# A convolution-and-gate block, forward and backward: g kept in SBUF, and forward spectra with real and imaginary parts on the partition rows

## The chip, the core and the metric

One Trainium2 chip, and one of its cores. The metric is the device time of one execution of the program in microseconds, from start to end. The kernel before took 626.39 us (median of 3 runs, 625.23 to 627.68).

## What is computed

The forward pass takes `x` (2048 rows of 512 numbers) through a layer norm, then through two branches whose results are multiplied:

```python
xn = layernorm(x)
K  = real(einsum("dn,dnl,dn->dl", C, exp(dt*A*l), dt*B))   # a filter of 2048 taps per channel
y  = irfft(rfft(pad(xn)) * rfft(pad(K)))[:2048]            # long convolution, one per channel
s  = y + xn * Dskip
g  = silu(silu(xn @ w1) @ w2)                              # w1 512 x 1792, w2 1792 x 512
out = x + s * g
```

The program returns `out` and the gradients of all inputs for a given `grad_out`. So backward passes follow: of the gate, of the two matrix products (`w1`, `w2`, and their input), of the convolution (by spectra again), of the filter's parameters, and of the layer norm.

## The kernel before, in words

**Blocks.** The 512 channels are four blocks `b` of 128. The convolution of a block uses discrete Fourier transforms of length 4096, written as matrix products in two steps. The forward transform is `dft_fwd` (L639): 32 matmuls with the table `TF` (L652), evacuations to SBUF (tile `dA`), 32 transposes (L661, or a transposing DMA), then the second step with the small table `F2` (L671). The inverse is `dft_inv` (L677): the table `I2` (L688), then `TI` (L696).

**Layout of a spectrum.** `F2` is a block of 64 output columns for the real part and 64 for the imaginary part. In the kernel before, L671 makes one part at a time, with 64 output columns, so that two such matmuls (`h` = 0 and 1) use the two column halves of TensorE's array. A spectrum then lies in SBUF as `[64 h + m, part, ...]`: both parts of a number on the same partition, beside each other in the free dimension. `I2` is applied with 64 contraction rows at a time (L688), two matmuls on the two row halves of the array.

**The forward convolution.** `gen_conv_x` (L887) makes the spectrum U of `xn` and stores it in DRAM (`Ud`). `gen_conv_fwd` (L896) loads the filter block `Kb`, makes its spectrum KX, loads U (`spectrum_in`, L881), stores KX (`KXd`), and forms the four products of parts in `cplx_parts` (L718): four instructions on VectorE (L722 to L725), whose four terms `dft_inv` adds up in PSUM. `consume` adds the skip term and makes S, which is stored (`Sd`, L917); the last block's S also stays on chip as `k.S_b`.

**Feed-forward and gates.** `gen_ffn_fwd` (L922) makes the two matrix products in 8 chunks of 256 rows (L936, L955). `gen_gate_rows` (L966) makes `g` = silu of a chunk (L990), stores it in DRAM (`Gd`, L991) and forms `ds` (gradient times g, L992); in a second pass it forms `do` (the gradient times the derivative of silu, L999 and L1000) and multiplies it by s of the first three blocks (L1002). The last block's columns are multiplied at L1550. `gen_out` (L1008) later loads S and g again and forms `x + s g` (L1029, L1030) beside the backward.

**Backward.** `gen_conv_bwd` (L1037) transforms `ds` forward (half-array matmuls as above), loads U and KX, multiplies with `cplx_mul` (L703: L707 to L712) and transforms back twice per block. `gen_ffn_da` (L1265) makes the gradients through w2 and w1 (L1298, L1308). Then come the gradients of the filter's parameters, of w2 (L1346) and of w1 (L1367).

**Order.** The program is first written as interleaved generators, which fixes buffers and dependencies. Then a planner (`Plan`, L36) takes all instructions, gives each a cost, and searches for an order on each engine: `solve` simulates the engines and DMA line with priorities from the last round (`back`), `search` (L386) repeats that with random weights and keeps the order with the earliest end, and `apply` nails it down. So an edit anywhere can move instructions everywhere. Each engine runs its list in order; SyncE (SP) issues most DMAs in order as well, and waits for a DMA's conditions hold up those behind it.

**Buffers.** The transforms draw on a pool with tags: `w8` (4 buffers of a spectrum), `t4` (2 buffers of half that; `Kb` and `S_b`) and `cm2` (1). A tile waits until the tile that had its buffer before has been used for the last time.

Of the kernel before, what the change touches and what calls it, by code (L numbers as in the profile page):

```python
# [24 lines left out]
BR, SR = 1.8, 0.5  # L25
# [10 lines left out]
class Plan:  # L36
# [3 lines left out]
    SEM, ROOM = 45.0, 212863  # L40

    def __init__(self, nc, tc):
# [69 lines left out]
        self.dma = ["DMA" in type(x).__name__ or "Dma" in type(x).__name__ for x in self.ins]  # L112

# [99 lines left out]
    def solve(self, age, pen=0.0, hold=None):  # L213
# [7 lines left out]
        line, tables = 0.0, "nesd"  # L221
# [22 lines left out]
        def pick(e):  # L244
            r = ready[e]
            if e != "Activation" or not pen:
                return heapq.heappop(r)[1]
            i = min(range(len(r)), key=lambda i: (r[i][0] + (pen if switch(r[i][1]) else 0.0), r[i][1]))
# [11 lines left out]
        while events:  # L260
# [110 lines left out]
    def search(self, rounds, seed):  # L371
# [5 lines left out]
        for _ in range(rounds):  # L377
            end = self.solve([-t for t in self.back()], draw.choice((2600.0, 4000.0, 6000.0)), end - draw.uniform(25000.0, 60000.0))
            if best is None or end < best[0]:
                best = end, self.plan, self.start  # L380
# [111 lines left out]
def make_consts(k, wp):  # L492
# [69 lines left out]
    k.I2n = const.tile([P, 128], BF16, name="I2n")  # L562
    TS(out=k.I2n[:], in_=k.I2[:, 0].rearrange("p c m -> p (c m)"), scalar=-1.0, op=ALU.mult)
# [77 lines left out]

def dft_fwd(k, w8, U, ev, dma=False):

# [22 lines left out]
    for u in range(2):  # L666
        for c in range(2):
# [9 lines left out]
def dft_inv(k, A2, Y, ev, consume, terms=None):  # L677
# [3 lines left out]
    terms = terms or [(Y[:, c], k.I2[:, c].rearrange("p c m -> p (c m)")) for c in range(2)]  # L681
    for q in range(4):
        ps = pc.tile([P, 2, 4, 32, 4], F32, name="ps_i2", tag="pc")
        for g in range(4):
            for c, (Yc, I2c) in enumerate(terms):
                for h in range(2):
                    hs = slice(64 * h, 64 * h + 64)
                    nc.tensor.matmul(out=ps[:, h, g], lhsT=Yc[hs, 4 * q + g, :], rhs=I2c[hs], start=(c == 0), stop=(c == len(terms) - 1))  # L688
# [27 lines left out]


def cplx_parts(k, w8, a, b):  # L718

    TT = k.nc.vector.tensor_tensor  # L720
    t = w8.tile([P, 16, P], BF16, name="cm4", tag="cm2")
    TT(out=t[:], in0=b[:, 0], in1=a[:, 0], op=ALU.mult)  # L722
    TT(out=b[:, 0], in0=b[:, 0], in1=a[:, 1], op=ALU.mult)
    TT(out=a[:, 0], in0=b[:, 1], in1=a[:, 0], op=ALU.mult)
    TT(out=b[:, 1], in0=b[:, 1], in1=a[:, 1], op=ALU.mult)  # L725
    re, im = (k.I2[:, c].rearrange("p c m -> p (c m)") for c in range(2))
    return [(t, re), (b[:, 0], im), (a[:, 0], im), (b[:, 1], k.I2n[:])]
# [153 lines left out]
def spectrum_in(k, w8, b, which):  # L881
    t = w8.tile([P, 2, 16, P], BF16, name="sp_in", tag="w8")
    k.nc.sync.dma_start(t[:].rearrange("p c g k -> p (c g k)"), {"U": k.Ud, "K": k.KXd}[which][b])
# [3 lines left out]
def gen_conv_x(k, b):  # L887
# [3 lines left out]
    U, _ = yield from dft_fwd(k, dft, lambda t: k.xn[:, t, bs], k.evc)  # L891
# [4 lines left out]
def gen_conv_fwd(k, b):  # L896
# [7 lines left out]
    KX, A2 = yield from dft_fwd(k, dft, lambda t: Kb[:, :, t, :], k.evc)  # L904
# [10 lines left out]
    yield from dft_inv(k, A2, U, k.evc, consume, terms)  # L915
    k.S_b = S
    (nc.scalar if b == 3 else nc.sync).dma_start(k.Sd[b], S[:].rearrange("p t d -> p (t d)"))  # L917
# [48 lines left out]
def gen_gate_rows(k, gp, lag):  # L966
# [5 lines left out]
    for t in range(0, k.T, 4):  # L972
        nc.sync.dma_start(Gr[:, t:t + 4, :], k.g_v[:, t:t + 4, :])
    rows, S = {}, {}

    def load_s(c):
        S[c] = gp.tile([P, 3, 2, P], BF16, name="S", tag="S", bufs=4)
        nc.sync.dma_start(S[c][:].rearrange("p b t d -> p b (t d)"), k.Sd[0:3, :, 256 * c:256 * c + 256].rearrange("b p n -> p b n"))
    for c in range(last):
# [9 lines left out]
        g = gp.tile([P, 2, k.D], BF16, name="g", tag="g", bufs=3)  # L989
        nc.scalar.activation(out=g[:], in_=rows[c], func=ACT.Silu)  # L990
        nc.sync.dma_start(k.Gd[:, ts, :], g[:])  # L991
        TT(out=k.ds[:, ts, :], in0=Gr[:, ts, :], in1=g[:], op=ALU.mult)  # L992
# [3 lines left out]
    for c in range(last):  # L996
# [4 lines left out]
        o3 = o[:, :, 0:3 * P].rearrange("p t (b d) -> p b t d", b=3)  # L1001
        TT(out=o3, in0=o3, in1=S.pop(c)[:], op=ALU.mult)  # L1002
# [5 lines left out]
def gen_out(k, pool):  # L1008
# [3 lines left out]
    n = k.T // 2  # L1012
    rows = lambda ap: ap.rearrange("p t (b d) -> p b t d", b=4)

    def load(c):
        ts = slice(2 * c, 2 * c + 2)
        S = pool.tile([P, 4, 2, P], BF16, name="go_s", tag="go_s", bufs=2)
        nc.sync.dma_start(S[:].rearrange("p b t d -> p b (t d)"), k.Sd[:, :, 256 * c:256 * c + 256].rearrange("b p n -> p b n"))
        g = pool.tile([P, 2, k.D], BF16, name="go_g", tag="go_g", bufs=2)
        nc.sync.dma_start(g[:], k.Gd[:, ts, :])  # L1020
        return S, g
    q = [load(0), load(1)]
    yield
    for c in range(n):
        S, g = q.pop(0)
        x = pool.tile([P, 2, k.D], BF16, name="go_x", tag="go_x", bufs=1)
        nc.sync.dma_start(x[:], k.x_v[:, 2 * c:2 * c + 2, :])
        yield
        TT(out=rows(g[:]), in0=rows(g[:]), in1=S[:], op=ALU.mult)  # L1029
        TT(out=x[:], in0=x[:], in1=g[:], op=ALU.add)  # L1030
        k.st(k.o0_v[:, 2 * c:2 * c + 2, :], x[:])
        if c + 2 < n:
            q.append(load(c + 2))
        yield


def gen_conv_bwd(k):  # L1037
# [10 lines left out]
    def rest(b):  # L1048
# [23 lines left out]
        yield from dft_inv(k, A2, KX, k.evc, consume_dx)  # L1072
        yield
# [191 lines left out]
def gen_ffn_da(k, da):  # L1265
# [11 lines left out]
    for c in range(T // 2):  # L1277
# [27 lines left out]
        for t in range(2):  # L1305
# [5 lines left out]
            if c >= DU_FIRST:  # L1311
                nc.vector.scalar_tensor_tensor(out=du, in0=ps[:], scalar=1.0, in1=du, op0=ALU.mult, op1=ALU.add,
# [112 lines left out]
def kernel(ctx, tc, A_u, A_A_re, A_A_im, A_B_re, A_B_im, A_C_re, A_C_im, A_log_dt, A_Dskip, B_x, B_w1, B_w2, grad_out,  # L1425
# [21 lines left out]
    k.Gd = dr.tile([P, 16, D], BF16, name="Gd")  # L1447
    k.Md = dr.tile([2 * NB, P, (NE + len(Y_EXP)) * 64], BF16, name="Md")
    k.Sd = dr.tile([NB, P, L], BF16, name="Sd")
# [24 lines left out]
    k.p1 = pool("p1", es=es_f)  # L1474
    k.fp = pool("fp", es=es_f)
    YD = pool("yd", side="right").tile([P, 8192], BF16, name="YD")
# [67 lines left out]
    es_g = es_x.enter_context(ExitStack())  # L1544
    gates = gen_gate_rows(k, pool("gate", side="right", es=es_g), 1)

    interleave([gen_conv_fwd(k, 3), ffn, gates], [1, 3, 1])
    for t in (slice(0, 8), slice(8, 16)):
        last = k.do[:, t, 3 * P:4 * P]
        nc.vector.tensor_tensor(out=last, in0=last, in1=k.S_b[:, t], op=ALU.mult)  # L1550
    es_f.close()
    es_g.close()
# [4 lines left out]
    es_o = es_d.enter_context(ExitStack())  # L1557
    go = pool("go", es=es_o)
    turned_in_place(k, k.W2, k.evw)
    bwd = gen_conv_bwd(k)  # L1560
    out = gen_out(k, go)
# [3 lines left out]
    paced(bwd, woven([ffb, out], [2, 1]), BR)  # L1565
    run(out)
    es_o.close()
# [12 lines left out]
    plan.search(27, 10)  # L1580
# [29 lines left out]
```

## Time and profile before

| | |
|---|---|
| median of 3 runs | 626.39 us |
| the profiled execution | 626.98 us, span 625.3 us, mean granted TensorE clock 0.983 |
| instructions in the profile | 15219 |
| DMA | 178884 packets, 149.63 MB, mean 239 GB/s |
| HBM | read 62.26 MB, written 61.47 MB |

How to read the profile: PE is the matmul side of TensorE, PEld its weight loads, DVE VectorE, ACT ScalarE, POOL GpSimd, SP SyncE. The span runs from the first to the last instruction, and the execution's own time holds 1.7 us more. A group's line gives the source line, engine, operation, what it writes and reads, the count, then the busy time in us and the mean of one in ns. A matmul's mean is its latency; matmuls follow each other at a shorter pace. The view of stages gives busy time per engine in a stretch of the span, with the granted clock and the DMA engines' busy share. The chain is followed back from the last instruction to what released each step.

### The profile page before, as it was taken

Reading aid. Unit: us, or ns where it says so; the run is one execution under the profiler, and the core shown is the slowest. Engines: PE = TensorE matmul, PEld = TensorE weight load, DVE = VectorE, ACT = ScalarE, POOL = GpSimd, SP = SyncE. Lnnn points to the kernel's source line nnn. Section 1 sums busy time; section 2 is a strip of 40 time slices with the busy share of each in tenths; the row PEclk is TensorE's granted clock in tenths of the full one; section 3 lists DMA queues with packets and bytes.
Section 4 is the critical chain, followed back from the end, with each engine's and each line's share of the span. In section 5 each row is a group of like instructions: output and inputs, shape, how many; then the busy total and the mean of one; then the engine's idle time right before and its main releaser. Section 6 shows DMA issues by size and latency. Waiting matters only on the chain.

```text
span 625.3 us, 15219 instructions
## 1 busy us (share of the span) xinstructions
PE 556.0 (89%) x6324; PEld 406.2 (65%) x6324; DVE 504.6 (81%) x881; ACT 459.5 (73%) x620; POOL 83.0 (13%) x157
## 2 busy tenths in 40 slices
PE   0158899889999999859999999999799999999997
PEld 0145665658577667556657665766677877776886
DVE  8999999989998733799979787964549798878692
ACT  6988978968989877996978786631867767663443
POOL 6521112010101010100000000010000302020134
PEclk9989999989999999998999999999899999999999
DMA  9574677798748497889699999999999999999973
GB/s 237 208 285 136 211 254 190 291 222 246 253 159 273 180 306 238 325 290 302 146 313 217 332 244 296 269 240 286 252 278 147 272 217 220 183 235 233 254 203 125
DMA packets 178884, 149.63 MB, mean 239 GB/s; under 512 B 105152, under 2 KB 157120, under 8 KB 175232
## 3 DMA queue, kind: packets, MB, share of 16 engines
q1 hardware_dynamic: 165776, 125.85, 75.0%
q0 software_dynamic: 6144, 17.83, 8.2%
q10 hardware_dynamic: 6896, 4.98, 2.6%
q8 instruction: 49, 0.80, 0.5%
q14 instruction: 19, 0.16, 0.1%
HBM read 62.26 MB, written 61.47 MB: 198 GB/s over the span
## 4 chain that ended last, share of the span: by engine, by line
PE 56%; DVE 19%; ACT 16%; DMA 5%; issue 3%; ACTq 1%; POOL 0%; SPq 0%; DVEq 0%
PE ps_w L1367 8%; PE ps_da L1298 7%; PE ps_dx L1308 7%; PE ps_w L1346 5%; ACT dA L402 3%; PE ps_i L688 3%; PE ps_h L936 3%; PE ps_o L955 3%; PE ps_s L671 3%; PE ps_s L652 2%; DVE Tp L1144 2%; PE ps_i L696 2%; PE ps_v L1134 2%; PE psS L1160 2%; PE psS L1156 2%
## 5 line engine op out<-in xcount | busy, mean ns | idle before, releaser
L402 ACT CAST dA<-ps_s 128x1024 bf16<-128x1024 f32 x96 | 95.5, 1040 | 13.9 <-PE ps_s L652 7.0
L936 PE MATMUL ps_h<-XT,W 128*128 128x256 bf16 x448 | 63.0, 282 | 7.2 <-DVE XT L403 5.2
L402 ACT CAST dB<-ps_i 128x1024 bf16<-128x1024 f32 x48 | 47.3, 1030 | 21.3 <-PE ps_i L688 21.1
L955 PE MATMUL ps_o<-W,aT 128*128 128x512 bf16 x224 | 57.0, 385 | 3.1 <-ACT aT L946 2.7
L1346 PE MATMUL ps_w<-YD,a_tok 128*128 128x512 bf16 x224 | 59.4, 379 | 0.0
L1298 PE MATMUL ps_da<-doT,W 128*128 128x256 bf16 x448 | 58.2, 278 | 0.0
L1144 DVE TENSOR_TENSOR Tp<-Vb,Eb 128x1344 bf16<-128x1344 bf16 x64 | 50.7, 852 | 9.1 <-ACT Vb L402 8.5
L1308 PE MATMUL ps_dx<-W,dhT 128*128 128x512 bf16 x224 | 56.2, 380 | 0.0
L936 PEld LDWEIGHTS <-W 128*128 128x128 bf16 x448 | 42.3, 101 | 18.8 <-issue 11.9
L402 ACT CAST Vb<-ps_v 128x672 bf16<-128x672 f32 x64 | 44.3, 743 | 9.7 <-PE ps_v L1134 9.1
L1298 PEld LDWEIGHTS <-W 128*128 128x128 bf16 x448 | 42.3, 99 | 10.9 <-issue 2.7
L1367 PEld LDWEIGHTS <-xn 128*128 128x128 bf16 x448 | 43.8, 98 | 5.3
L1300 DVE TENSOR_TENSOR dhT<-ps_da,dhT 128x512 bf16<-128x512 f32 x56 | 38.0, 686 | 10.4 <-PE ps_da L1298 6.5
L402 ACT CAST o<-ps_w 128x256 bf16<-128x256 f32 (+1 forms) x42 | 18.7, 446 | 33.9 <-PE ps_w L1367 26.3
L1274 ACT ACTIVATE dhT<-dhT 128x2048 bf16<-128x2048 bf16 (+1 forms) x16 | 27.2, 1713 | 15.9 <-DMA dhT<-Hd 8.5
L947 POOL DMA_DIRECT2D Hd<-hT x16 | 16.4, 1023 | 166.8 <-ACT hT L402 166.8
L652 PEld LDWEIGHTS <-TF 128*128 128x128 bf16 x384 | 27.2, 103 | 16.5 <-issue 8.5
L688 PEld LDWEIGHTS <-sp_in 64*128 64x128 bf16 x768 | 27.8, 94 | 15.3 <-issue 8.5
L955 PEld LDWEIGHTS <-aT 128*128 128x128 bf16 x224 | 19.7, 99 | 24.3 <-ACT aT L946 5.7
L402 ACT CAST hT<-ps_h 128x512 bf16<-128x512 f32 x56 | 31.9, 622 | 4.7 <-PE pt_f L661 3.0
L688 PE MATMUL ps_i<-I,sp_in 64*128 64x128 bf16 x640 | 34.0, 218 | 0.9 <-ACT dK L402 0.6
L1308 PEld LDWEIGHTS <-dhT 128*128 128x128 bf16 x224 | 20.0, 98 | 21.9 <-issue 3.7
(237 smaller groups left out, 1325.8 us busy)
## 6 DMA issues: line engine op xcount, KB each, us to landing
Yd<-YD SPq DMA_DIRECT2D x8, 1024.0 KB, 8.4
sp_in<-Ud SPq DMA_DIRECT2D x8, 1024.0 KB, 7.9
h_in<-Hd SPq DMA_DIRECT2D x14, 512.0 KB, 4.8
Ed<-E SPq DMA_DIRECT2D x8, 672.0 KB, 4.5
Eb<-Ed SPq DMA_DIRECT2D x8, 672.0 KB, 5.7
Hd<-hT POOLq DMA_DIRECT2D x8, 512.0 KB, 6.2
Ud<-dA SPq DMA_DIRECT2D x4, 1024.0 KB, 4.8
KXd<-dA SPq DMA_DIRECT2D x4, 1024.0 KB, 5.2
```

The costliest lines, as they stand in the source:

```text
L402: return self.nc.scalar.copy(out=out, in_=in_)
L652: nc.tensor.matmul(out=ps[:, j], lhsT=k.TF[:, 8 * h + j, c, :], rhs=U(8 * h + j), start=True, stop=True)
L688: nc.tensor.matmul(out=ps[:, h, g], lhsT=Yc[hs, 4 * q + g, :], rhs=I2c[hs], start=(c == 0), stop=(c == len(terms) - 1))
L936: nc.tensor.matmul(out=ps[:, j], lhsT=k.W1[:, dk, ft * P:ft * P + P], rhs=XTv[:, :, dk, :], start=(dk == 0), stop=(dk == DK - 1))
L955: nc.tensor.matmul(out=ps[:], lhsT=aT[:, ft, t * P:t * P + P], rhs=k.W2[:, ft, :], start=(ft == 0), stop=(ft == FT - 1))
L1144: k.nc.vector.tensor_tensor(out=Tp[:, c, :, r ^ c].rearrange("p e (q w) a -> p q w e a", w=2), in0=Vb[:, :, c].rearrange("p q w (e a) -> p ...
L1274: nc.scalar.activation(out=dh[:, 0:n], in_=dh[:, 0:n], func=ACT.Derivative_silu)
L1298: nc.tensor.matmul(out=ps[:, j], lhsT=k.W2[:, ft, dk * P:dk * P + P], rhs=dTv[:, :, dk, :], start=(dk == 0), stop=(dk == DK - 1))
L1300: nc.vector.tensor_tensor(out=dh[:, i0:i0 + 2, :], in0=ps[:], in1=dh[:, i0:i0 + 2, :], op=ALU.mult)
L1308: nc.tensor.matmul(out=ps[:], lhsT=dhs[ft // 8][:, ft % 8, t * P:t * P + P], rhs=k.W1[:, :, ft * P:ft * P + P], start=(ft == 0), stop=(ft ...
L1346: nc.tensor.matmul(out=ps[:], lhsT=at[:, t, :], rhs=k.do[:, t, :], start=(t == 0), stop=(t == k.T - 1))
L1367: nc.tensor.matmul(out=ps[:], lhsT=k.xn[:, t, dk * P:dk * P + P], rhs=dh[:, t].rearrange("p j n -> p (j n)"), start=(t == 0), stop=(t == k ...
```

## The change

- **Spectra.** With `packed`, the second step of `dft_fwd` applies all 128 columns of `F2` at once: 8 matmuls of 128 x 128 instead of 16 of 128 x 64. The result has the real part on partitions 0 to 63 and the imaginary part on 64 to 127. The forward transforms of `xn` and of the filter use it; those of `ds` in the backward don't.
- **Products.** KX, U and a copy of U with the two partition halves swapped (`sp_sw`, four loads per block from DRAM, tag `t4`) are multiplied elementwise, again in four instructions on VectorE. `dft_inv` then adds two terms of 128 contraction rows, with `I2d` (`I2` with the sign of the lower half turned) and `I2`, instead of four terms of 64 rows twice. The new `I2d` replaces `I2n`; `cplx_parts` goes.
- **Loads in the backward.** `spectrum_in` brings the stored spectra back into the old layout, with four loads of 64 partitions each instead of one of 128.
- **g and s.** g stays in SBUF (`g8`, new pool `go`). The second gate pass multiplies both `do` and `g8` by s, `finish_rows` does so for the last block's columns and adds x; `gen_out`, the DRAM tensor `Gd` and the last block's store of S go.
- **Planner.** Its costs of half-array matmuls change, it counts 96 ns for a change of PE's tiling, it may prefer matmuls of the present tiling, and it searches 50 rounds with another seed. `BR`, a weight in the interleaving, goes from 1.8 to 1.0. The pools `fp` and `p1` change their order.

```diff
-BR, SR = 1.8, 0.5
+BR, SR = 1.0, 0.5
...
+    def tiling(x):
+        rows, cols = x.tile_size
+        return 0 if rows * cols == P * P else 1 if rows < P else 2
...
-            half = x.tile_size[0] * x.tile_size[1] < P * P
-            return (d if not half else 3.0 if sum(x.tile_position) == 0 else d + 20.0), d + 165.0
+            if self.tiling(x):
+                return (3.0 if sum(x.tile_position) == 0 else 0.487 * self.count(aps[0]) - 10.0), d + 165.0
+            return d, d + 165.0
...
+                    if self.mode[n] != mode:
+                        mode, d, l = self.mode[n], d + self.TURN, l + self.TURN
...
-    k.I2n = const.tile([P, 128], BF16, name="I2n")
-    TS(out=k.I2n[:], in_=k.I2[:, 0].rearrange("p c m -> p (c m)"), scalar=-1.0, op=ALU.mult)
+    k.I2d = const.tile([P, 128], BF16, name="I2d")
+    for p0, sign in ((0, 1.0), (64, -1.0)):
+        TS(out=k.I2d[p0:p0 + 64], in_=k.I2[p0:p0 + 64, 0].rearrange("p c m -> p (c m)"), scalar=sign, op=ALU.mult)
...
+        for v in range(2 if packed else 0):
+            ps = pc.tile([P, 8, P], F32, name="ps_s2", tag="pc")
+            for h in range(2):
+                nc.tensor.matmul(out=ps[:, 4 * h:4 * h + 4], lhsT=k.F2[:].rearrange("p c m -> p (c m)"), rhs=Bv[:, u, v, h],
+                                 start=True, stop=True)
+            ev(A[:, u, 8 * v:8 * v + 8, :], ps[:])
...
+            for h in range(2 if terms else 0):
+                for i, (T, w) in enumerate(zip(terms(q // 2), (k.I2d[:], I2[1]))):
+                    nc.tensor.matmul(out=ps[:, h, g], lhsT=T[:, 8 * (q % 2) + 4 * h + g, :], rhs=w, start=(i == 0), stop=(i == 1))
...
-    k.nc.sync.dma_start(t[:].rearrange("p c g k -> p (c g k)"), {"U": k.Ud, "K": k.KXd}[which][b])
+    src = {"U": k.Ud, "K": k.KXd}[which][b].rearrange("(c m) (q h n) -> c h m q n", c=2, q=4, h=2)
+    for c in range(2):
+        for h in range(2):
+            k.nc.sync.dma_start(t[64 * h:64 * h + 64, c].rearrange("p (q g) k -> p q (g k)", q=4), src[c, h])
...
-    U = spectrum_in(k, dft, b, "U")
+    U = dft.tile([P, 2, 16, P], BF16, name="sp_in", tag="w8")
+    Us = [dft.tile([P, 16, P], BF16, name="sp_sw", tag="t4") for u in range(2)]
+    for u in range(2):
+        us = slice(2048 * u, 2048 * u + 2048)
+        nc.sync.dma_start(U[:, u].rearrange("p g k -> p (g k)"), k.Ud[b][:, us])
+        for p0 in (0, 64):
+            nc.sync.dma_start(Us[u][p0:p0 + 64].rearrange("p g k -> p (g k)"), k.Ud[b][64 - p0:128 - p0, us])
...
-    terms = cplx_parts(k, dft, KX, U)
+    for u in range(2):
+        nc.vector.tensor_tensor(out=U[:, u], in0=U[:, u], in1=KX[:, u], op=ALU.mult)
+        nc.vector.tensor_tensor(out=Us[u][:], in0=Us[u][:], in1=KX[:, u], op=ALU.mult)
...
-    (nc.scalar if b == 3 else nc.sync).dma_start(k.Sd[b], S[:].rearrange("p t d -> p (t d)"))
+    if b < 3:
+        nc.sync.dma_start(k.Sd[b], S[:].rearrange("p t d -> p (t d)"))
...
-        g = gp.tile([P, 2, k.D], BF16, name="g", tag="g", bufs=3)
-        nc.scalar.activation(out=g[:], in_=rows[c], func=ACT.Silu)
-        nc.sync.dma_start(k.Gd[:, ts, :], g[:])
+        g = k.g8[:, ts, :]
+        nc.scalar.activation(out=g, in_=rows[c], func=ACT.Silu)
...
-        o3 = o[:, :, 0:3 * P].rearrange("p t (b d) -> p b t d", b=3)
-        TT(out=o3, in0=o3, in1=S.pop(c)[:], op=ALU.mult)
+        s3 = S.pop(c)
+        for r in (o, k.g8[:, ts, :]):
+            r3 = r[:, :, 0:3 * P].rearrange("p t (b d) -> p b t d", b=3)
+            TT(out=r3, in0=r3, in1=s3[:], op=ALU.mult)
...
+def finish_rows(k, go):
+    for rows in (k.do, k.g8):
+        for t in (slice(0, 8), slice(8, 16)):
+            last = rows[:, t, 3 * P:4 * P]
+            TT(out=last, in0=last, in1=k.S_b[:, t], op=ALU.mult)
+    for c in range(k.T // 2):
+        x = go.tile([P, 2, k.D], BF16, name="go_x", tag="go_x", bufs=2)
+        nc.sync.dma_start(x[:], k.x_v[:, ts, :])
+        TT(out=x[:], in0=x[:], in1=k.g8[:, ts, :], op=ALU.add)
+        k.st(k.o0_v[:, ts, :], x[:])
...
-    plan.search(27, 10)
+    plan.search(50, 1)
```

More of the change, by code (lines that the diff above doesn't have):

```diff
@@ L211, in graph, with solve @@
         self.ahead = succ, begun, wait, groups
-    def solve(self, age, pen=0.0, hold=None):
+    def solve(self, age, pen=0.0, hold=None, turn=0.0):
         N = len(self.ins)
@@ L220, in solve @@
         free = dict.fromkeys(ready, 0.0)
-        line, tables = 0.0, "nesd"
+        line, tables, mode = 0.0, "nesd", 0
         heat, warm = {}, {0: False}
@@ L245, in pick @@
             r = ready[e]
-            if e != "Activation" or not pen:
+            if e == "Activation" and pen:
+                i = min(range(len(r)), key=lambda i: (r[i][0] + (pen if switch(r[i][1]) else 0.0), r[i][1]))
+            elif e == "PE" and turn and self.mode[r[0][1]] != mode:
+                i = min(range(len(r)), key=lambda i: (r[i][0] + (turn if self.mode[r[i][1]] != mode else 0.0), r[i][1]))
+            else:
                 return heapq.heappop(r)[1]
-            i = min(range(len(r)), key=lambda i: (r[i][0] + (pen if switch(r[i][1]) else 0.0), r[i][1]))
             n = r[i][1]
@@ L377, in search @@
         for _ in range(rounds):
-            end = self.solve([-t for t in self.back()], draw.choice((2600.0, 4000.0, 6000.0)), end - draw.uniform(25000.0, 60000.0))
+            end = self.solve([-t for t in self.back()], draw.choice((2600.0, 4000.0, 6000.0)), end - draw.uniform(25000.0, 60000.0),
+                             draw.choice(self.PEN))
             if best is None or end < best[0]:
@@ L680, in dft_inv @@
     out = A2[:].rearrange("p c t (q h g e) -> p q (h g) (c t) e", q=4, h=2, e=4)
-    terms = terms or [(Y[:, c], k.I2[:, c].rearrange("p c m -> p (c m)")) for c in range(2)]
+    I2 = [k.I2[:, c].rearrange("p c m -> p (c m)") for c in range(2)]
     for q in range(4):
@@ L1072, in rest @@
         yield from dft_inv(k, A2, KX, k.evc, consume_dx)
+        k.du_done = b == 3
         yield
@@ L1543 @@
     k.late = True
-    es_g = es_x.enter_context(ExitStack())
-    gates = gen_gate_rows(k, pool("gate", side="right", es=es_g), 1)
+    go = pool("go", side="right", es=es_x)
+    es_r = es_x.enter_context(ExitStack())
+    gates = gen_gate_rows(k, pool("gate", side="right", es=es_r), go, 1)
     interleave([gen_conv_fwd(k, 3), ffn, gates], [1, 3, 1])
-    for t in (slice(0, 8), slice(8, 16)):
-        last = k.do[:, t, 3 * P:4 * P]
-        nc.vector.tensor_tensor(out=last, in0=last, in1=k.S_b[:, t], op=ALU.mult)
+    finish_rows(k, go)
     es_f.close()
-    es_g.close()
+    es_r.close()
     base = dft_pool("dftb", es_x, {"cm2": 1, "w8b": 2}, k.dft, side="right")
@@ L1564 @@
     ffb = gen_ffn_da(k, da)
-    paced(bwd, woven([ffb, out], [2, 1]), BR)
-    run(out)
-    es_o.close()
+    paced(bwd, ffb, BR)
     es_x.close()
```

65 lines of the change are left out of this document (17 added, 48 removed).

## The prediction

> **What bounds the kernel now.** I read the busy shares first, then the chain that ended last, then both by stage.
>
> ```profile
> PE 556.0 (89%) x6324; PEld 406.2 (65%) x6324; DVE 504.6 (81%) x881; ACT 459.5 (73%) x620; POOL 83.0 (13%) x157
> ...
> PE   0158899889999999859999999999799999999997
> ...
> PEclk9989999989999999998999999999899999999999
> ...
> PE 56%; DVE 19%; ACT 16%; DMA 5%; issue 3%; ACTq 1%; POOL 0%; SPq 0%; DVEq 0%
> ```
>
> TensorE (PE) is the busiest engine, yet only 56% of the chain is PE. So the next view is busy time by stage:
>
> ```profile
> core 0: us, PE busy (x) PEld busy (x) DVE busy (x) ACT busy (x) POOL busy (x), PEclk, DMA share, GB/s
> 45.00:195.00 150.00, 136.56 (x1663) 98.58 (x1662) 141.74 (x193) 129.89 (x183) 15.40 (x15) 0.98 0.68 214
> 195.00:223.00 28.00, 27.77 (x320) 18.61 (x319) 20.16 (x27) 25.73 (x35) 2.85 (x4) 1.00 0.71 259
> 223.00:282.00 59.00, 49.24 (x676) 36.30 (x675) 36.14 (x50) 52.55 (x68) 3.68 (x5) 0.98 0.86 287
> 282.00:430.00 148.00, 146.79 (x1608) 98.90 (x1606) 122.56 (x181) 99.80 (x106) 5.43 (x10) 0.98 0.99 263
> 430.00:573.00 143.00, 136.88 (x1557) 103.19 (x1556) 109.34 (x250) 93.77 (x134) 18.23 (x34) 0.99 1.02 229
> ```
>
> From 282 us on (backward passes) PE is full: what PE saves there, the kernel saves. From 45 to 195 us three engines share the load and DVE (141.74 of 150) is fuller than PE. From 195 to 223 PE is full. From 223 to 282, where the last block's convolution, the gates and the turn to the backward meet, ACT is the fullest. The chain says the same, stage by stage:
>
> ```profile
> by line: PE ps_h L936 9.0%; PE ps_o L955 7.9%; ACT dA L402 7.6%; DMA XT<-xn 5.8%; ACT sn L808 5.7%; PE pt_f L661 3.7%; PE ps_s L652 3.6%; issue 3.6%; DVE YD L828 3.5%; DVE AR L826 3.5%; DVE m L827 3.5%; PE ps_k L842 3.4%; ACT hT L402 3.4%;
> by line: PE ps_o L955 23.0%; PE ps_h L936 17.1%; PE ps_s L671 15.8%; PE ps_k L842 13.7%; PE pt_f L661 12.8%; PE ps_s L652 8.0%; ACT aT L946 6.5%; ACT hT L402 4.2%; issue 1.3%; ACT Xr L402 0.1%; ACTq L402 0.1%
> by line: ACT YD L999 13.0%; DMA YD<-Od 12.6%; ACT g L990 10.6%; ACT aT L946 10.4%; ACT dA L402 8.4%; ACT L999 6.5%; ACT dB L402 6.2%; DMA Kd<-KE 6.2%; issue 5.6%; ACTq L877 4.5%; ACT hT L402 4.4%; ACT L990 4.3%; ACT KE L402 4.3%; ACT ob L40
> ```
>
> These are 45–195, 195–223 and 223–282. PE entries sum to 27.6% in the first (9.0+7.9+3.7+3.6+3.4; the line is cut, so it is a lower bound), 90.4% in the second, nothing visible in the third.
>
> **Full-array matmuls: what they save.** Pieces of the chain in order of time (start, us, what):
>
> ```profile
> 361.68 0.16 PE ps_i L688 x2
> 361.85 0.21 PE ps_da L1298
> 362.06 0.94 PE ps_i L688 x30
> ...
> 365.28 1.79 PE ps_i L696 x32
> ...
> 374.36 0.55 PE ps_s L671 x4
> ...
> 376.11 0.54 PE ps_dx L1308 x2
> ...
> 413.26 5.89 PE ps_da L1298 x54
> 419.15 6.04 PE ps_dx L1308 x28
> ```
>
> The paces of full-array matmuls: L696 1.79/32 = 56 ns at 128 columns, L1298 5.89/54 = 109 ns at 256, L1308 6.04/28 = 216 ns at 512. Now the half-array ones. L671 uses half the columns and runs as pairs: 4 of them are two pairs, 2 x 0.216 = 0.43 us, but take 0.55; and two ps_dx ahead of such a run take 0.54 instead of 0.43. Going into half arrays and back costs 0.12 + 0.11 = 0.23 us. L688 uses half the rows: 30 are 15 pairs, 0.84 us at 56 ns, but take 0.94; the one ps_da ahead of it takes 0.21 instead of 0.11. Together 0.20 us per visit. So a half-array pair costs what one full matmul costs, and the arithmetic saves nothing: the diff puts one full matmul (L684, L707 of the new file) where a pair stood. What it saves is the visits.
>
> In the instruction order of the two built programs PE visits half arrays 92 times before (44 of L671's kind, 48 of L688's) and 38 times after (13 and 25), all 38 in the backward. By place, from the order and the start times: 17 and 9 visits in 45–195, 17 x 0.23 + 9 x 0.20 = 5.7 us; 8 and 0 in 195–223, 1.8 us; 3 and 9 in 223–282, 2.5 us; 16 and 30 after 282, of which 13 and 25 stay, 3 x 0.23 + 5 x 0.20 = 1.7 us. All of it is 11.7 us of PE time.
>
> What of it reaches the end: after 282 all, 1.7 (PE full). In 195–223, 90% of 1.8: 1.6. In 45–195 between 27.6% of 5.7 (1.6) and all of it (PE busy 91%, but so is DVE 94%): I take 1.6, because DVE is the fuller engine. In 223–282 nothing to 2.5; I take 0: the chain is ACT there.
>
> **The last block and SP's queue.** Timeline, 244 to 262 us:
>
> ```profile
> 246.93 2.60 SPq L991 DMA_DIRECT2D Gd<-g  x2
> ...
> 249.63 0.58 SPq L883 DMA_DIRECT2D sp_in<-Ud  x1
> ...
> 258.18 1.23 DVE L722 TENSOR_TENSOR cm<-sp_in,dA 128x2048 bf16<-128x2048 bf16 x1 [2.91 <-DMA sp_in<-Ud]
> ```
>
> Before, SP held the last block's load of U 2.6 us behind stores of g that waited for ACT; the product on DVE then waited 2.91 us for that load. With g on chip those stores go. After, i2 can also start when one half's two products are done, not all four. But the loads double: U, and U again with its halves swapped. Prices of the nearest DMAs (KB each, us to landing):
>
> ```profile
> sp_in<-Ud SPq DMA_DIRECT2D x8, 1024.0 KB, 7.9
> ...
> Gd<-g SPq DMA_DIRECT2D x8, 256.0 KB, 5.8
> ...
> go_s<-Sd SPq DMA_DIRECT2D x8, 256.0 KB, 5.3
> ```
>
> Six pieces of 256 to 512 KB instead of one of 1024 KB land between as before (7.9) and twice that (15.8); against it stand 2.6 us and, since the swapped loads wait only for earlier users of their two buffers, an earlier issue. Ends: 2.6 won, 7.9 lost. I take 0, as ACT's queue of Silu and its derivative sets this stretch and not the product. The Trainium skill, page "DMA: Bandwidth & Descriptors", section "Rules for kernel authors", speaks against the change here: it advises not to split a transfer into two partition halves, as they share the same engines and serialize. By it the 15.8 would hold, 7.9 more; no trace here shows the split.
>
> In the backward the same doubt meets 8 loads of spectra, now four pieces of 256 KB each: 7.9 to 4 x 5.3 = 21 us if one after the other. I take 7.9, the row of the same bytes; the cover is ps_da and ps_dx, which keep PE at 146.79 of 148, and without that cover the worst end is 13 us on one load.
>
> **g and s on chip.** Removed: 8 stores and 8 loads of g and 8 loads of s, 256 KB each, and the last block's store of s, 512 KB: 6,656 KB; added 4 x 1,024 KB for the swapped U. SP issues grow by 20 + 24 and shrink by 24. DVE's rows:
>
> ```profile
> L1030 DVE TENSOR_TENSOR go_x<-go_x,go_g 128x1024 bf16<-128x1024 bf16 x8 | 5.5, 683 | 0.0
> L1029 DVE TENSOR_TENSOR go_g<-go_g,go_s 128x1024 bf16<-128x1024 bf16 x8 | 5.5, 683 | 0.7 <-DMA go_g<-Gd 0.7
> L1002 DVE TENSOR_TENSOR YD<-YD,S 128x768 bf16<-128x768 bf16 x8 | 4.3, 549 | 1.2 <-DMA S<-Sd 1.2
> L1550 DVE TENSOR_TENSOR YD<-YD,S_b 128x1024 bf16<-128x1024 bf16 x2 | 1.4, 682 | 0.0
> ```
>
> The 8 products L1029 (5.5 us), spread over the backward, become 8 like L1002 and 2 like L1550 (4.3 + 1.4 = 5.7 us) around the turn. There DVE is busy 36.14 of 59 us, so 23 us of idle hide them; without that cover they cost 5.7. The additions L1030 stay. In the backward DVE had 25 us of idle, so the lighter load gives nothing.
>
> **Sum.** 1.7 + 1.6 + 1.6 = 4.9 us off. The profiled execution took 626.98 us (span 625.3 and 1.7 around it), 0.6 above the median 626.39; so about 622.1 for a like execution and **621.5** for the median. Its own range: 618 to 624.
>
> **Rivals.**
> (a) PE bounds the forward too, since DVE's and ACT's waits there are partly for PE in-order work: all 11.7 us count. 626.4 - 11.7 = 614.7. For it: PE 91% busy in 45–195. Against: DVE 94%.
> (b) The forward is DVE's and ACT's, and only the backward's 1.7 counts: 624.7. For it: the third chain line; against: 90% PE in 195–223.
> (c) The clock. One row shows it at half, after a thin stretch:
>
> ```profile
> 276.00:280.00 4.00, 1.57 (x19) 1.25 (x19) 4.00 (x7) 3.97 (x5) 0.00 (x0) 0.96 0.77 238
> 280.00:286.00 6.00, 4.89 (x33) 3.78 (x31) 5.98 (x12) 6.00 (x7) 0.00 (x0) 0.50 1.00 313
> ```
>
> After 4 us in which PE was busy for 1.57, the granted clock was 0.50 for 6 us: 3 us of work lost. A forward with less PE work could bring one more such stretch: 621.5 + 3 = 624.5. The Trainium skill, "TensorE: Matmul & The Clock Gate", "Why this matters for your kernels", says that an idle window of about 3 us halves the clock; this row agrees, and one more window is not certain.
> (d) Slower: SP's queue, which is in order, stalls on the swapped loads. They wait for buffers that the K block, the swapped U and S share (two buffers), and behind them stand loads that DVE and PE need: in the new order, first of all E's store and the magnitudes of the next tables. Two rows price such a stall, one of SP's waits and one of the chain:
>
> ```profile
> SPq L901 <- DMA Kd<-KE: 46.0, 4, 19.5
> ...
> 97.25 8.70 DMA XT<-xn
> ```
>
> One load that came late cost the chain 8.70. With (b)'s gain, 624.7 + 8.7 = 633; with mine 630. It decides once a swapped load holds SP past the time when DVE runs out of table work. Against it: in 45–195 DVE was idle for only 8 of 150 us, whatever it waited for, with as strict a queue.
> (e) That it doesn't do what it says: the instruction order shows the 54 visits gone, so only their worth is open.
>
> **Chances.** Forecast 0.42, (a) 0.18, (b) 0.17, (c) 0.08, (d) 0.15. The range of 612 to 631 holds all but half of (d) and the tails. A measurement tells 0.5% (3.1 us) from no change: faster means below 623.3, slower above 629.5. Forecast (less a tail of 0.02) and (a) are faster, 0.58; (b), (c) and that tail the same, 0.27; (d) slower, 0.15.
>
> **What would show it.** Right: PE pieces of 56 ns for L707 with no step ahead of them; PE busy lower by about 11 us; the first ps_da 3 us earlier; the backward 1.7 us shorter. Wrong: the product waiting longer than 2.91 us for sp_in or sp_sw; DVE waiting for tables' loads behind the swapped loads; first ps_da no earlier though PE's busy time fell (b); the first ps_da 9 us earlier (a); more half-clock stretches (c).

## The result and the profile after

| | before | after |
|---|---|---|
| runs side by side, median (lowest to highest of 7) | 627.38 us (625.23 to 628.65) | 621.92 us (619.05 to 628.40) |
| ratio, 95% interval | | 0.992 (0.989 to 0.995) |
| profiled execution, span, mean granted clock | 626.98 us, 625.3 us, 0.983 | 621.48 us, 619.8 us, 0.989 |

The forecast was 621.5 us. The changed kernel was timed twice more beside the kernel before (below as c1_after and c2_after): 0.9964 (0.9936 to 0.9992) and 0.9965 (0.9932 to 0.9999). Ratios, here and below, are of the runs in the faster of two states that executions show, medians and ranges of all runs. The three intervals lie below 1, the third only just. So the gain is small, 0.4 to 0.8% by the ratios, some 3 us in their mean; by the medians of the three sets it is 5.5, 1.4 and 0.9 us. Two sets of three lie below the 0.5% that the prediction set as its bound. The number was met; its composition wasn't, as the rest shows.

First the profile page of the kernel after: busy time, PE's and the clock's rows of forty slices, and the chain.

```profile
PE 541.0 (87%) x5958; PEld 407.7 (66%) x6004; DVE 503.3 (81%) x884; ACT 457.8 (74%) x620; POOL 79.7 (13%) x157
...
PE   0139999888999988969999899799999999999998
...
PEclk9999999999999997989999999999999999999999
...
PE 52%; DVE 18%; ACT 15%; DMA 10%; issue 3%; ACTq 1%; POOL 0%; SPq 0%; DVEq 0%
```

PE is 15.0 us less busy, but 46 matmul records are missing here (5958 against 6004 weight loads). The profile of the second repeat, c2_after, has them all:

```profile
PE 544.7 (88%) x6004; PEld 407.8 (66%) x6004; DVE 503.5 (81%) x884; ACT 457.6 (74%) x620; POOL 78.1 (13%) x157
```

Against 556.0 before that is 11.3 us less PE time; 11.7 was predicted. In the chain DMA's share rose from 5% to 10%. The view of stages of after, with bounds moved to its own landmarks (columns as before):

```profile
43.00:193.00 150.00, 138.06 (x1542) 105.47 (x1558) 147.17 (x202) 135.33 (x193) 13.94 (x17) 1.00 0.82 252
193.00:221.00 28.00, 26.78 (x335) 21.41 (x339) 20.95 (x27) 27.46 (x45) 2.27 (x3) 1.00 0.79 257
221.00:276.00 55.00, 43.14 (x477) 33.20 (x478) 37.26 (x55) 46.57 (x52) 2.81 (x4) 0.92 0.93 275
276.00:436.00 160.00, 153.01 (x1664) 104.78 (x1663) 124.08 (x183) 101.93 (x108) 6.51 (x12) 0.99 1.02 230
436.00:567.00 131.00, 125.54 (x1469) 95.71 (x1489) 102.42 (x241) 91.27 (x132) 17.10 (x32) 1.00 1.04 227
```

The first stage is as long as before, starts 2 us earlier and is fuller (DVE 147.17 of 150 us, 141.74 before); the third is 4 us shorter. The fourth has become longer: PE, which was busy for 146.79 of 148 us in the backward before, is now idle for 7 of 160. The turn is easiest to see between two instructions that both kernels have, the first `ps_da` (backward through w2) and the last `ps_dx`. Between them, before and then after:

```profile
282.50:438.20 155.70, 154.49 (x1654) 103.24 (x1653) 124.90 (x185) 100.17 (x106) 5.98 (x11) 0.99 1.00 264
```

```profile
275.40:436.20 160.80, 153.81 (x1667) 105.27 (x1667) 124.88 (x185) 102.53 (x108) 6.51 (x12) 0.98 1.02 229
```

So the backward starts 7.1 us earlier (3.2 predicted) and takes 5.1 us longer (1.7 shorter predicted). Part of the 5.1 is a border: 14 more weight loads lie in this stretch (x1667 for x1653), and the stretch behind it has as many fewer. It is cleaner to take all from the first `ps_da` to the end: 342.8 us before (625.3 - 282.5), 344.4 after (619.8 - 275.4). The rest is PE waiting for DMAs, in the chain of waits of after (276 to 436 us; start, us, what):

```profile
by line: PE ps_da L1311 24.6%; PE ps_dx L1321 22.9%; DMA dhT<-Hd 10.1%; PE ps_i L711 7.0%; DMA Pd<-pd_s 6.5%; PE ps_i L719 4.5%; issue 3.6%; PE ps_s L691 3.1%; PE ps_s L666 2.6%; DVE dhT L1313 1.9%; DVE sp_in L732 1.8%; PE pt_f L675 1.4%; A
...
330.71 8.23 DMA dhT<-Hd
...
339.45 7.90 DMA dhT<-Hd
...
383.39 10.38 DMA Pd<-pd_s
```

### The profile page after: what moved, and what is told of

Read it like the earlier page. It is cut to its first block, busy times and chain, and to the rows that moved or that the text cites. A ratio compares the mean times of both kernels' runs of the same rounds, so it can differ in the third digit from the quotient of the medians.

```text
span 619.8 us, 14576 instructions
## 1 busy us (share of the span) xinstructions
PE 541.0 (87%) x5958; PEld 407.7 (66%) x6004; DVE 503.3 (81%) x884; ACT 457.8 (74%) x620; POOL 79.7 (13%) x157
## 4 chain that ended last, share of the span: by engine, by line
PE 52%; DVE 18%; ACT 15%; DMA 10%; issue 3%; ACTq 1%; POOL 0%; SPq 0%; DVEq 0%
PE ps_w L1381 8%; PE ps_da L1311 6%; PE ps_dx L1321 6%; ACT dA L415 5%; PE ps_w L1360 5%; PE ps_o L978 4%; PE ps_h L959 3%; DMA dhT<-Hd 3%; DMA Kd<-KE 2%; PE psS L1169 2%; PE ps_v L1147 2%; PE ps_i L711 2%; DVE Tp L1157 2%; PE psS L1173 2%; DMA Pd<-pd_s 2%
## 5 line engine op out<-in xcount | busy, mean ns | idle before, releaser
L415 ACT CAST dA<-ps_s 128x1024 bf16<-128x1024 f32 x96 | 94.1, 1056 | 8.4 <-PE ps_s L691 4.2
L959 PE MATMUL ps_h<-XT,W 128*128 128x256 bf16 x448 | 61.5, 285 | 5.9 <-ACT ob L415 3.3
L415 ACT CAST dB<-ps_i 128x1024 bf16<-128x1024 f32 x48 | 47.6, 1028 | 11.8 <-PE ps_i L711 8.6
L978 PE MATMUL ps_o<-W,aT 128*128 128x512 bf16 x208 | 52.8, 379 | 2.3 <-ACT hT L415 1.0
L1360 PE MATMUL ps_w<-YD,a_tok 128*128 128x512 bf16 x202 | 53.3, 379 | 0.8
L959 PEld LDWEIGHTS <-W 128*128 128x128 bf16 x448 | 43.9, 102 | 14.6 <-issue 6.4
L1311 PEld LDWEIGHTS <-W 128*128 128x128 bf16 x448 | 42.6, 99 | 15.3 <-issue 7.2
L1287 ACT ACTIVATE dhT<-dhT 128x2048 bf16<-128x2048 bf16 (+1 forms) x16 | 27.1, 1704 | 13.3 <-DMA dhT<-Hd 13.3
L970 POOL DMA_DIRECT2D Hd<-hT x16 | 14.0, 876 | 150.6 <-ACT hT L415 150.6
L1147 PE MATMUL ps_v<-Gb,YT 128*128 128x168 bf16 x256 | 29.6, 236 | 2.6 <-DMA YT<-Yd 1.1
L819 ACT ACTIVATE sn<-AR 128x2048 bf16<-128x2048 int32 (+1 forms) x16 | 30.5, 1912 | 1.8 <-DVE AR L817 1.8
```

Of the source, the lines that this page charges most:

```text
L415: return self.nc.scalar.copy(out=out, in_=in_)
L819: nc.scalar.activation(out=sn[:, :, 0:n], in_=V[:, :, 0:n], func=ACT.Sin, scale=-2 * PI_LO / 2.0 ** 32)
L959: nc.tensor.matmul(out=ps[:, j], lhsT=k.W1[:, dk, ft * P:ft * P + P], rhs=XTv[:, :, dk, :], start=(dk == 0), stop=(dk == DK - 1))
L978: nc.tensor.matmul(out=ps[:], lhsT=aT[:, ft, t * P:t * P + P], rhs=k.W2[:, ft, :], start=(ft == 0), stop=(ft == FT - 1))
L1147: nc.tensor.matmul(out=ps[:, u, 168 * c:168 * c + 168], lhsT=YT[:, c, q + u, :], rhs=Gb[:, q0 + q + u].rearrange("p w x -> p (w x)"), star ...
L1287: nc.scalar.activation(out=dh[:, 0:n], in_=dh[:, 0:n], func=ACT.Derivative_silu)
```

## Experiments

The theory at first: the visits to half arrays give the gain, at the price and with the shares of the prediction; the backward's loss comes from how its spectra are loaded, or from the order. The rivals: all PE time counts (a); the order that the planner happened to find gives the difference; the removed transfers matter after all.

All results in one table. "Visits" are PE's visits to half arrays ahead of the first `ps_da`, from the instruction order. "First ps_da", "from there" (to the end) and "PE idle" (between first `ps_da` and last `ps_dx`) are of the profiled execution, in us. Ratios are to the kernel before on the same chip; its medians in the three sets were 625.81 (first four rows below c2_after), 625.89 (c1_after, e5 to e7) and 625.61 (c2_after, e8 to e10).

| kernel | visits | first ps_da | from there | PE idle | median | ratio (95%) |
|---|---|---|---|---|---|---|
| before | 46 | 282.5 | 342.8 | 1.2 | | 1 |
| after | 0 | 275.4 | 344.4 | 7.0 | 621.92 | 0.992 (0.989, 0.995) |
| c1_after | 0 | 278.9 | 344.2 | 5.5 | 624.46 | 0.9964 (0.9936, 0.9992) |
| c2_after | 0 | 274.9 | 346.2 | 7.9 | 624.67 | 0.9965 (0.9932, 0.9999) |
| e1_halves | 25 | 276.8 | 349.7 | 7.0 | 628.20 | 1.0034 (1.0015, 1.0053) |
| e2_long | 0 | 274.4 | 345.7 | 6.3 | 621.00 | 0.9937 (0.9903, 0.9971) |
| e3_seed | 0 | 278.8 | 351.6 | 8.1 | 631.37 | 1.0074 (1.0047, 1.0102) |
| e4_planner | 41 | 280.7 | 346.3 | 3.3 | 628.77 | 1.0057 (1.0033, 1.0082) |
| e5_dma | 0 | 275.2 | 354.7 | 15.0 | 629.08 | 1.0054 (1.0029, 1.0080) |
| e6_seed4 | 0 | 285.1 | 339.2 | 3.7 | 623.24 | 0.9964 (0.9940, 0.9987) |
| e7_bseed2 | 50 | 294.1 | 345.2 | 3.0 | 643.23 | 1.0281 (1.0247, 1.0315) |
| e8_halves | 25 | 279.2 | 348.0 | 8.5 | 628.21 | 1.0039 (1.0011, 1.0067) |
| e9_spec | 0 | 273.9 | 349.5 | 9.4 | 623.30 | 0.9957 (0.9932, 0.9982) |
| e10_g | 41 | 297.1 | 336.5 | 2.9 | 635.10 | 1.0132 (1.0100, 1.0163) |

**What a visit costs: e1_halves and e8_halves.** In the order of after, kept as it is, each full matmul of L684 becomes the pair of half-array matmuls that stood there before. The planner plans the first of a pair alone; the second is put behind it when the order is nailed down.

```diff
-                nc.tensor.matmul(out=ps[:, 4 * h:4 * h + 4], lhsT=k.F2[:].rearrange("p c m -> p (c m)"), rhs=Bv[:, u, v, h],
-                                 start=True, stop=True)
+                for c in range(2):
+                    TWINS[c].append(nc.tensor.matmul(out=ps[64 * c:64 * c + 64, 4 * h:4 * h + 4], lhsT=k.F2[:, c, :], rhs=Bv[:, u, v, h],
+                                                     start=True, stop=True))
...
+            line = [y for n in line for y in ([self.ins[n], self.twin[n]] if n in self.twin else [self.ins[n]])]
```

> The kernel after, with its own order of instructions on every engine, in which only the 64 full-array matmuls of the packed second step (L684) are each put back as a pair of half-column matmuls. PE then visits half arrays 25 more times, all in the forward. At 0.23 us a visit that is 5.8 us of PE time. Theory (a visit counts where the chain is on PE): 9 of the 25 places lie on the chain of the kernel after, so about 2 us longer than after, 624. Rival A (PE bounds the whole forward): 5.8 us longer, 627.7. Rival N (visits were hidden anyway, and the new order alone brought the gain): within 0.5 us of after, 622.

> The first experiment again (the kernel after, its own order, 64 matmuls put back as pairs of half-column ones, 25 visits more), this time beside the kernel after itself on the same chip; the two were measured in different sets before, 1.0034 against 0.992 and 0.9964. The traces show each visit at 0.22 us and the first ps_da 1.4 us later. Theory (a visit counts where the chain is on PE): 2 us slower than after in this set. Rival A (all visits count): 5.5 us slower or more.

The same stretch of PE's order, first in c2_after and then in e8_halves, which ran on the same chip (timeline: start, us, what; a group's time runs to its last end, so the pace is read from start to start):

```profile
209.15 0.56 PE L675 MATMUL pt_f<-band,dA 128*128 128x128 bf16 x7
209.54 0.59 PE L684 MATMUL ps_s<-dB,F 128*128 128x512 bf16 x2
209.97 1.25 PE L959 MATMUL ps_h<-XT,W 128*128 128x256 bf16 x10
```

```profile
211.82 0.55 PE L682 MATMUL pt_f<-band,dA 128*128 128x128 bf16 x7
212.31 0.62 PE L692 MATMUL ps_s<-dB,F 128*64 128x512 bf16 x4
212.86 1.27 PE L967 MATMUL ps_h<-XT,W 128*128 128x256 bf16 x10
```

Seven transposes take 0.39 us ahead of full matmuls and 0.49 ahead of half ones; two full matmuls take 0.43 us, the two pairs that do the same work take 0.55. That is 0.10 + 0.12 = 0.22 us per visit, and a pair costs one full matmul. So the price was right (0.23). The Trainium skill, "TensorEngine Tiling (Array Packing)", "Key Properties", says that a change of tiling mode drains TensorE; these two steps agree. For 25 visits it makes 5.5 us of PE time. Of it, 3.5 us reach the end by the medians of one set (628.21 - 624.67) and 4.6 by the two ratios (1.0039 - 0.9965, of 626). In e8_halves 15 of the visits stand ahead of 193 us, 6 between 193 and 221 and 4 behind; by the shares of the prediction (28%, 90%, nothing) 2.1 us would reach the end. The two intervals together leave 4.6 +/- 2.7, so this one pair of runs excludes neither the 2.1 nor all 5.5. e1_halves, the same kernel in another set, gave the same ratio (1.0034), and the three ratios of after lie at 0.992 to 0.9965. The profiles don't say where the cost arises either: from c2_after to e8_halves the first `ps_da` comes 4.3 us later and the rest takes 1.8 us longer, from after to e1_halves it is 1.4 and 5.3, though all 25 visits lie ahead of the first `ps_da`. So the visits do cost time at the end; whether a share of it, as predicted, or all, as in rival (a), these runs don't decide.

**How the backward's spectra are loaded: e2_long.** The loads stay four, but each row of DRAM comes as one run of 4 KB instead of four of 1 KB; the rows' contents stand in another order then.

```diff
-    src = {"U": k.Ud, "K": k.KXd}[which][b].rearrange("(c m) (q h n) -> c h m q n", c=2, q=4, h=2)
+    src = {"U": k.Ud, "K": k.KXd}[which][b].rearrange("(c m) (h q n) -> c h m q n", c=2, q=4, h=2)
```

> The kernel after, with its own order, in which the backward's loads of spectra read runs of 4 KB in place of 1 KB (same number of loads, same bytes, same buffers; the spectra then stand in a wrong order, so the backward's numbers differ). After has 7 us of PE idle between 340 and 436 us that before hasn't, behind late loads of dhT and stores of pd_s. Theory (runs of 1 KB keep the DMA engines busy longer and make the others late): PE idle there falls to 2 us or less, and the time by about 5 us, 617. Rival (the new order of DMA issues makes them late, whatever the runs): same time as after within 1 us.

The ratio is 0.9937, PE's idle time in the backward 6.3 us against 5.5 to 7.9: the length of the runs is not what holds PE. That the spectra come in 32 transfers instead of 8 was not tried by itself.

**The removed transfers: e5_dma.** Into after's order, 21 of the removed transfers are put back beside the backward: seven stores of g (256 KB), seven loads of g (256 KB) and seven of S (192 KB), 4,928 KB in all. Nothing reads what they load.

```diff
+        for d in range(max(c - 1, 0), c):
+            ds = slice(2 * d, 2 * d + 2)
+            TWINS.append(nc.sync.dma_start(k.Gd[:, ds, :], k.g8[:, ds, :]))
+            old = go.tile([P, 2, k.D], BF16, name="go_g", tag="go_g", bufs=1)
+            TWINS.append(nc.sync.dma_start(old[:], k.Gd[:, 0:2, :]))
+            old = go.tile([P, 3, 2, P], BF16, name="go_s", tag="go_s", bufs=1)
+            TWINS.append(nc.sync.dma_start(old[:].rearrange("p b t d -> p b (t d)"), k.Sd[:, :, 256 * d:256 * d + 256].rearrange("b p n -> p b n")))
```

> The kernel after, with its own order, in which seven of the eight sets of DMAs that the change removed are put back into the backward, each behind a load of x: the store of a chunk of g (256 KB, of the product in this kernel), a load of g (256 KB) and a load of s (192 KB), into buffers that nothing reads. That is 21 DMAs, 4.9 MB. Theory (these DMAs are off the path, as the prediction costed them at nothing): within 1 us of after. Rival (the backward's DMA engines are full, and the 7 us of PE idle there come from late transfers, so 4.9 MB more lengthen it): 5 us or more longer, 627 or above.

> The kernel after once more, unchanged, as the mark for the others of this set on their chip. Both theories: 0.992 of before, within the interval of the first measurement, 0.989 to 0.995.

They cost 5.6 us by the two ratios (1.0054 - 0.9964, of 626; the intervals together leave 5.6 +/- 2.4) and 4.6 by the medians (629.08 - 624.46, the control on the same chip). The control itself, c1_after, came out at 0.9964, outside the 0.989 to 0.995 that was expected. The waits of the backward (us in total, times, longest), first after, then e5_dma:

```profile
ACT dhT L1287 <- DMA dhT<-Hd: 13.3, 6, 4.6
...
ACT pd_s L415 <- DMA Pd<-pd_s: 4.1, 1, 4.1
```

```profile
ACT dhT L1300 <- DMA dhT<-Hd: 23.5, 6, 8.0
...
DVE cm L736 <- DMA sp_in<-Ud: 7.8, 2, 6.0
...
DVE cm L736 <- DMA sp_in<-KXd: 5.6, 2, 3.4
```

Where ACT waited 13.3 us for the stored activations (11.8 in c1_after) it now waits 23.5, and the loads of spectra come late as well; PE's idle time goes to 15.0 us. The stretch between the two landmarks is 172.2 us long, 11.6 more than in c1_after, though it began 3.7 us earlier. First c1_after, then e5_dma:

```profile
278.90:439.50 160.60, 155.15 (x1666) 106.37 (x1666) 125.06 (x185) 102.58 (x108) 6.51 (x12) 0.97 1.00 229
```

```profile
275.20:447.40 172.20, 157.19 (x1666) 107.21 (x1666) 125.64 (x185) 102.57 (x108) 6.51 (x12) 0.96 1.03 243
```

The DMA share is 1.03 here and was 1.00 without the extra bytes (1.02 in the profile of after): the DMA engines had no room left, and transfers that no engine waits for still cost time. Other loads land later, as dhT of 512 KB, after 7.1 us in the median against 6.1 in c1_after. A second way stays open: SP issues the 21 in its own order, at some 0.4 us each, and waits five times for one of them to land (us in total, times, longest):

```profile
SPq L1055 <- DMA Gd<-g: 3.2, 1, 3.2
SPq L1057 <- DMA go_s<-Sd: 2.7, 2, 2.0
SPq L1055 <- DMA go_g<-Gd: 1.9, 2, 1.0
```

What stands behind them in SP's queue starts later for that; the runs don't part the two. (This profiled execution took 631.65 us, 2.6 above its kernel's median.)

**The order's luck: e3_seed, e6_seed4, e4_planner, e7_bseed2.** The first two are after with another seed (2, and 4 in e6_seed4):

```diff
-    plan.search(50, 1)
+    plan.search(50, 2)
```

The last two are before with all planner edits of the change and seed 1, or 2 in e7_bseed2:

```diff
-    plan.search(27, 10)
+    plan.search(50, 1)
```

> The kernel after with another seed of the planner's search (2 in place of 1): another order of the same work; 39 visits to half arrays in place of 38. Theory (the gain is in the work that goes): 622 within 3 us, below before in any case. Rival (the gain of 5.5 us is the luck of one order): it may come out at 627 or above.

> The kernel after with seed 4 of the planner's search (40 visits, none in the forward). With seed 2 it was 1.5% slower than with seed 1. Theory now (an order's luck is some 5 us either way, the removed work some 5 to 6 us on the average): between 622 and 632. Rival (seed 1 is typical and seed 2 was the odd one): 622 within 2 us.

> The kernel before with the planner of after (its costs of half arrays, 96 ns for a change of tiling, preference, 50 rounds, seed 1) and nothing else of the change. Visits fall from 92 to 73 (44 to 35 and 48 to 38), 9 x 0.23 + 10 x 0.20 = 4.1 us of PE time, of which 5 and 0 before the first ps_da. Theory (visits count in full only in the backward, in part in the forward): 2 to 3 us faster than before, 624 to 625. Rival (the planner brought the whole gain): 622 or below. Rival (an order's luck outweighs it): 627 or above.

> The kernel before with the planner of after and seed 2 (92 visits, 50 of them in the forward). Theory (removed work on top of an order's luck): like seed 1 of this pairing (1.0057 of before), slower than the mean of the kernel after's seeds: 627 to 637. Rival (the work that goes is worth nothing, all is luck): as fast as the kernel after's seeds, 622 to 627.

The same work in three orders (after, e3, e6) takes 0.992 to 1.0074 of the time; the work of before under the new planner takes 1.0057 and 1.0281. One draw moves the time by as much as the whole change does, and within it the stages trade: e6_seed4 comes to the first `ps_da` at 285.1 us, 6 to 10 us after the other two, and has the shortest rest (339.2). The 7.1 and 5.1 us of the result are inside that spread. The planner by itself shows no gain: both draws are slower than before with its own order. e3_seed and e4_planner went the way of the rival that an order's luck outweighs the change; e6_seed4 lies in both of its ranges; e7_bseed2, at 643.23 us, is slower than the 627 to 637 of its expectation.

**One part alone: e9_spec and e10_g.** Both are before with after's planner and seed 1: e9_spec with the spectra's part (`packed`, products, loads), e10_g with g's (`g8`, `finish_rows`, `BR`, pools).

> The kernel before with the planner of after (seed 1) and the spectra's part of the change alone: full-array matmuls and the swapped loads, while g and s still go through DRAM and the last step beside the backward reads them back. 35 visits, none in the forward. The same planner without it gave 1.0057 and 1.0281 of before with two seeds, the whole change 0.994, 1.0074 and 0.9964 with three. Theory (the visits carry most of the gain): 0.993 to 1.003. Rival (g's DMAs, which are still there, carry it): 1.005 to 1.02.

> The kernel before with the planner of after (seed 1) and g's part of the change alone: g stays on chip and s g is formed at the second gate pass, while the spectra keep the old layout and half-array matmuls. 72 visits, 41 in the forward. Theory (the visits carry most of the gain, and g's DMAs matter only in the order of after): 1.002 to 1.015. Rival (g's DMAs carry it): 0.99 to 1.0.

> The kernel after once more, unchanged, as the mark for this set. So far it stood at 0.992 and at 0.9964 of before in two sets. Both theories: 0.992 to 0.997.

e9_spec is as fast as the whole change (0.9957 beside 0.9965 in the same set); e10_g is slower than before. Sort the kernels by whether their forward visits half arrays: without visits (after, e3, e6, e9) the first `ps_da` comes at 275.4, 278.8, 285.1 and 273.9 us, 278.3 in the mean; with them (before, e4, e7, e10) at 282.5, 280.7, 294.1 and 297.1, 288.6 in the mean. That is 10.3 us for 41 to 50 visits, which at 0.22 us are 9 to 11. From there to the end it is 346.2 us in the mean without and 342.7 with them. Four orders on each side with a spread of 11 and 16 us make that likely, not proved. g's part alone shows no gain in its one draw, although 21 of its transfers cost 5.6 us when they are put back into after's order. One draw each, against a spread of 1.1 to 1.5% between draws of the same work, doesn't rank the two parts.

## Why the prediction was right, and where not

The time was met with steps that were off in opposite directions.

- **The price of a visit** (0.23 and 0.20 us) and the sum of PE time (11.7) held: 0.22 and 11.3. Ahead of the first `ps_da` PE was busy for 223.75 us in before and 213.19 in c2_after, 10.6 less (10.0 predicted), behind it for 332.22 and 331.52, 0.7 less (1.7 predicted). Not all of it is visits: before ran 16 more `ps_h` in the first 45 us, at a pace of 0.21 us instead of 0.11, which makes an estimated 1.6 of the 10.6. Matmuls of the new L707 run at 56 ns with no step, as in this piece of after's chain (0.67/12):

```profile
130.55 0.67 PE ps_i L707 x12
```

- **What reaches the end ahead of the turn (1.6 + 1.6 + 0) was too small.** The first `ps_da` came 7.1, 3.6 and 7.6 us earlier in the three profiles of after, not 3.2. The step that failed is "I take 1.6, because DVE is the fuller engine": in after's first stage DVE was busy for 147.17 of 150 us instead of 141.74, as if part of its idle time had been PE's. That would be rival (a)'s mechanism, for the forward alone, and is argued: the order changed too, in a kept order 25 visits moved the first `ps_da` by 1.4 and 4.3 us, and e6_seed4, without visits, comes to it at 285.1 us, later than before.
- **The backward (1.7 won) has the wrong sign.** From the first `ps_da` on, after needs 1.4 to 3.4 us more than before in its three profiles. "PE full, so all counts" took a stage's occupancy for a bound that would stay; DMA, at a share of 0.99 there, was as full, and PE arrived earlier at it.
- **Removed DMAs at zero** was wrong: e5_dma prices 21 of them at 5.6 us in after's order (4.6 by the medians).
- **The spectra in four pieces at zero** holds for the loads themselves, with the 7.9 us of the prediction. After's row for them, and an issue of four on SP:

```profile
sp_in<-Ud SPq DMA_DIRECT2D x16, 256.0 KB, 6.0
...
sp_in<-KXd SPq DMA_DIRECT2D x16, 256.0 KB, 5.1
```

```profile
334.83 2.67 SPq L897 DMA_DIRECT2D sp_in<-Ud  x4
```

  Four issues take 2.67 us. In after's eight loads the last piece lands 7.4 to 10.4 us after the first issue, 8.1 in the median: near the predicted 7.9, not 21. One whole load in before's backward took 5.2 to 7.8 us, 6.4 in the median, so the four pieces are slower by an estimated 1.7 us. The Trainium skill, "DMA: Bandwidth & Descriptors", "Rules for kernel authors", says that two transfers to disjoint partition halves serialize. A doubling, as the prediction worked out from it for the last block, is not what these loads show. Whether 32 transfers instead of 8 are what lets PE wait longer in every order with packed spectra (3.7 to 9.4 us idle) than in every order without (1.2 to 3.3) stays open: these orders also start the backward earlier, the other explanation, all but e6_seed4, which has the 3.7.
- **The last block, 0,** held. Waits for U ahead of the turn, in before (43 to 282 us) and in after (43 to 276):

```profile
DVE cm L722 <- DMA sp_in<-Ud: 7.3, 2, 4.4
```

```profile
DVE sp_in L929 <- DMA sp_in<-Ud: 2.9, 2, 2.2
```

  No product waits for a swapped load; rival (d) did not come. SP did wait 9.5 us at these loads (5.5 for a store of S, 4.0 for PE), but DVE was busy for 147.17 of 150 us all the same.
- **Rival (c), the clock.** Between 48 us and the last 3 us of the span the clock stood at half for 13.6 us in before, 13.6 in after and 23.8 in c1_after. The prediction takes its row at the turn as agreeing with an idle window of about 3 us. The row doesn't show one: PE was busy for 1.57 of 4 us, its longest gap ahead of the half clock is 1.51 us, and the clock halved all the same. At the turn, after and then c1_after (the column with 0.51 and 0.52 is the granted clock):

```profile
273.80:280.80 7.00, 5.45 (x36) 4.33 (x36) 6.46 (x13) 7.00 (x8) 0.00 (x0) 0.51 1.27 224
```

```profile
274.00:284.60 10.60, 8.41 (x60) 6.89 (x61) 9.83 (x18) 10.57 (x11) 0.00 (x0) 0.52 1.25 241
```

  The same program, so such stretches come and go between executions. The 10.2 us more are 5 us of work, and c1_after's span was 3.3 us longer than after's.
- **The step that the prediction lacked is the order.** It counted the change as edits to one fixed order, while the planner made a new one. The draws above span 1.1 to 1.5% of the time for after's work and 2.8% for before's, more than the 0.8% that was forecast: with the same mechanisms another seed would have given "slower" (e3_seed). The range of 612 to 631 was argued from other causes; after's two other draws lie in it (623.24) and just outside (631.37). That 621.5 was met to 0.4 us is therefore luck in part.

What is shown: 0.22 us per visit on PE, a cost of 25 visits at the end in a kept order (4.6 +/- 2.7 us), 5.6 +/- 2.4 us for 21 transfers, and the spread of the draws. What is argued: that the spectra's part carries the gain (e9_spec beside e10_g and the grouping). Open: how much of the 3 us is the order, and why the backward of after loses time.

## What to carry to other kernels

Price a change of tiling by its visits, not by its matmuls: a pair of half-array matmuls costs one full one, and 0.22 us go for entering and leaving. A stage where PE is full may be one where DMA is just as full, and then neither PE time that is saved nor transfers that nobody waits for can be counted by PE's row alone. Where a search sets the order, first time a few seeds of the kernel as it stands: here they spread by more than the change is worth, and an edit is told from luck only in a kept order or over several seeds.

## What was not expected of the hardware

- The DMA engines' share was 1.02 in the backward of after at 229 GB/s and 1.00 in that of before at 264: full at both, with 13% fewer bytes per second.
- The half-clock stretches are not a property of the program alone: three profiles of one program had 13.6, 23.8 and 13.6 us at half clock in the stretch named above. Its times go with the clock: of the twelve executions of c2_after, five with a mean granted clock of 0.989 or more took 620.83 to 622.83 us, seven with 0.986 or less took 624.18 to 629.85. In the 29 executions of before beside it there is no such order (622.93 us at 0.983, 629.87 at 0.989). So a part of what parts after's three sets may be how often such a stretch came; why before shows no such tie is open.
